# A transformer-mixer prompt kernel: the first chunk's weights and queries, two-matmul dense steps in layer 0, and newly annealed orders of all engines

## The chip, the core and the metric

The kernel runs on one core of a Trainium2 chip. The metric is the device time of one execution in microseconds (us). The engines are TensorE (PE; its weight loads are listed as PEld), VectorE (DVE), ScalarE (ACT), GpSimd (POOL), and SyncE (SP), which issues every DMA of this kernel. Each engine runs its own list of instructions in order and waits on semaphores for the others.

## What is computed

Two equal layers, each with an attention block (A) and a token-mixing MLP (B), on 2048 tokens of width 512, in bf16:

```
def _A_ref(x, wqkv, wo):      # H = 32 heads of 16, window W = 256
    qkv = (x @ wqkv) ...
    scores = einsum("bhqd,bhkd->bhqk", q, k) * Dh ** -0.5
    mask = (i - j >= 0) & (i - j < W)
    p = softmax(where(mask, scores, -1e9))
    return (p @ v) @ wo
def _B_ref(x, w1, b1, w2, b2): # F = 1792
    u = gelu(einsum("bsd,sf->bdf", layernorm(x), w1) + b1)
    return transpose(einsum("bdf,fs->bds", u, w2) + b2)
x = x + _A_ref(layernorm(x)); x = x + _B_ref(layernorm(x))   # twice
```

The MLP mixes tokens: its first matmul sums over all 2048 tokens, its second makes all of them again.

## The kernel before, in words

The tokens are cut into four chunks of 512 (four tiles of 128 each). A chunk is *prepared* (`prepare`, L1052): layer norm statistics on DVE (L686, L688), the inverse root on POOL (L691, L693), normalization on DVE (L697), four PE transposes per tile (L747), whose result DVE or ACT copies out (L731, L733), and then `qkv` (L727): K and Q by `proj` (L756, matmuls at L764, four of 128x512 for each of four blocks o of eight heads), V by `vproj` (L785, 16 small matmuls for each of four sub-blocks, L794). K is written out as `kbd`, two masked copies: in chunk 0 straight by ACT (L773), elsewhere through `stg` and POOL (L780). Q's copy `qT` is a DVE or ACT eviction (L731, L733).

`attention` (L826) takes the four blocks o of a chunk one after the other. For each it makes four (chunk 0) or five *pieces*. A piece is one group of score matmuls (L848, 8 or 12 matmuls in 32-row tiles), two ACT exps of 128x1024 (L860), and masks on DVE (L873, L876). Below, a *step* is one piece, counted from 0; a layer has 76 of them. When a block's pieces are done, a group of 72 or 112 matmuls multiplies the probabilities with V (PV, L894). DVE copies its two banks (`cs`, L938); then follows a normalization by DMA: SP gathers the denominators (L940), copies half the result to other partitions (four DMAs, L944), DVE takes the reciprocal (L947), SP writes it to DRAM (L949) and reads it back spread over partitions (`md`, L952), and POOL multiplies (`oT`, L956). The last block of the last chunk takes a direct path through PE and ACT.

`wo_block` (L962) multiplies the four `oT` of a chunk by `wo` (L966), DVE adds to x, and a twofold layer norm follows. `u_part` (L998) is the MLP's first matmul, one chunk of tokens at a time, added up in SBUF by DVE (L1021, L1024), with GELU on ACT in its last part (L1027); it streams w1 in 256 KB pieces (L981). `y_block` (L1032) is the second matmul (L1035) with w2 (L992). Layer 1's chunks are prepared from `y_block`s of layer 0. The part of the kernel that is neither score nor PV is called *dense*; it fills PE between score groups.

What runs when is fixed while the program is built. `Graph.op` records each operation with its readers, writers and a cost. `schedule` (L350) with `_pick` (L264) is a list scheduler: it places operations on engines by readiness, priority and `RANK`, and inserts warm-up matmuls (L613). Then `reorder` (L420) shifts operations by the offsets in `MOVES` (L35), and `emit` (L429) writes each engine's list with the waits that it needs. A dense group is cut into operations of `STEP` = 4 matmuls (L704, `mm_group` L714, and `u_part`); between two such operations the order may place something else. Each operation signals once, after its last matmul. The last part of `u_part` has steps of one matmul.

SP's list opens with four tiles of x (128 KB each), the 512 KB of V weights, 512 KB of x, K's first 128 KB block, 512 KB of x, Q's first 128 KB block, then the rest.

Of the kernel before, what the change touches and what calls it, by code (L numbers as in the profile page):

```python
# [13 lines left out]
SWITCH = 100.0  # L14
# [6 lines left out]
RANK = (  # L21
    -18, 0, -107, -93, 7, 6, -38, -55, -48, 11, -107, 10, 37, -42, 7, 0, -4, -7, 17, -3, -66, 62, -49, 17, 1, 15,
    -19, 14, -13, 0, 6, 0, -51, 35, 0, 0, 0, 0, 7, -6, 0, 0, 15, 19, -6, -31, 0, -13, -3, 399, 0, 49, -23, 0, -1,
    18, 8, 17, 226, 11, -1, -10, -4, 7, 6, -31, -47, 105, 10, 0, 0, 15, -362, 42, 322, -14, -380, 0, -24, 52, 33,
    -20, -38, -11, 40, 51, -19, 55, -55, 11, 0, 0, 142, -1, 10, -5, 23, 2, 0, 44, 4, 41, 164, 28, -29, 0, 31, 0, 1,
    -46, 60, 13, 0, -18, 0, 15, 8, -122, 460, -486, -53, 10, -5, 0, 7, -20, -3, -14, 0, 12, 0, -12, 1, 0, 0, 0, 0,
    0, -52, 0, 0, 0, 0, 0, 0, 0, 49, -6, -6, -13, -155, -126, 185, -106, -33, -165, 6, -9, 0, -137, -4, 10, 2, 152,
    260, 114, 69, 200, -193, 10, 17, -14, 0, 6, -188, 4, 8, 15, -2, 0, 17, -15, 11, 17, 0, 0, -6, -79, -112, -156,
    0, -15, -114, 238, 115, -376, -10, 2, 0, 17, 0, 4, 6, 12, 0, -28, 0, 0, 117, 31, -17, -17, 0, 0, 473, -6, 86,
    -9, -3, -9, -384, -150, -479, 217, 122, 0, 36, 157, 53, 18, -27, 0, -6, 0, 38, 0, 1, 50, 52, 12, 14, 193, -18,  # L30
    13, 0, -11, 0, 113, 408, -134, 107, -30, -22, -52, 0, 14, 163, 38, 0, 186, -153, -439, 359, -7, 0, -3, 15, -10,
    13, 10, -109, 5, 0, 18, -105, -52, -43, 17, -46, -58, -33, -135, -167, -266, 232, 53, -39, 1, 2, 4, -16, 0, -18,
    -39, 0, 0, 3, 0, -1, 0, 0, 0, 0, 0, 0, 0, 0, 0, 0, 0, 0, 0, 0, 0, 0, 0, 0, 0, 0, 0, 0, 6,
# [3 lines left out]
        3, -1, 2, 5, -2, -4, 0, -2, 1, 3, 1, -1, 1, -6, 0, 0, 0, 0, 1, 1, -2, 0, 1, -1, 0, 0, 0, 0, 2, -1, -1, 1,  # L37
        -1, 0, 1, 1, -2, 2, 0, -2, 0, 0, 0, 2, -1, 1, 3, -3, -1, -1, 0, 0, 0, 0, 0, 0, 0, 0, 0, 0, 0, 0, 0, 0, 0, 0,
        0, 0, 0, 1, -1, 0, 0, 0, 1, -1, 0, 0, 0, 0, 0, 0, 0, 0, 0, 0, 0, 0, 0, 0, 1, -1, 0, 0, 0, 0, 0, 0, 0, 0, 0,
        0, 0, 0, 0, 0, 0, 0, 0, 0, 0, 0, 0, 0, 0, 0, 0, 0, 0, 0, 1, -1, 0, 0, 0, 1, -1, 0, 0, 0, 0, 0, 0, 0, 0, 0,  # L40
        0, 0, 0, 0, 0, 0, 0, 0, 0, 0, 0, 0, 0, 0, 0, 0, 0, 0, 0, 1, -1, 0, 0, 0, 0, 0, 0, 0, 0, 0, 0, 0, 0, 0, 0, 0,
        0, 0, 0, 0, 0, 0, 0, 0, 0, 0, 0, 0, 0, 0, 0, 0, 0, 0, 0, 0, 0, 0, 0, 0, 0, 0, 0, 0, 1, -1, 0, 0, 0, 0, 0, 0,
        0, 0, 0, 0, 0, 0, 0, 0, 0, 0, 0, 0, 0, 0, 0, 0, 0, 0, 0, 0, 0, 0, 0, 0, 0, 0, 0, 0, 0, 0, 0, 0, 0, 0, 1, 1,
        3, 1, -4, -2, 0, 5, 1, 2, 0, -4, 1, -5, 1, 8, 0, 2, 2, 5, -6, -4, 3, -2, 2, -7, -4, 0, 3, 3, 3, -3, 2, -4,
        -4, 0, 0, 0, 21, 21, -1, 2, 2, 2, -6, 1, 3, 3, -8, -8, -8, 4, 4, -2, 7, 2, -4, 1, -5, 3, -6, -14, 1, 1, -16,
        0, 0, 0, 0, 0, 0, 0, 0, 0, 0, 1, -1, 0, 0, 0, 0, 1, -1, 0, 0, 0, 1, 1, -2, 0, 0, 0, 1, 2, -2, -1, 0, 0, 1,
        -1, 0, 0, 0, 0, 0, 0, 1, 1, -2, 0, 0, 0, 0, 0, 0, 0, 0, 0, 0, 0, 0, 0, 0, 0, 0, 0, 0, 0, 0, 0, 0, 1, -1, 0,
        0, 0, 0, 0, 0, 0, 0, 0, 0, 0, 0, 1, -1, 0, 0, 1, -1, 0, 1, -1, 1, -1, 1, -1, 0, 0, 0, 0, 0, 0, 0, 0, 0, 0,
        0, 0, 0, 0, 0, 0, 0, 0, 0, 0, 0, 0, 0, 0, 0, 0, 0, 0, 0, 2, 0, -2, 0, 0, 0, 0, 0, 0, 0, 0, 0, 0, 0, 0, 0, 1,
        -1, 0, 2, 3, -2, -2, -1, 0, 0, 0, 0, 0, 0, 0, 0, 1, -1, 0, 0, 0, 0, 0, 0, 0, 0, 0, 0, 0, 0, 0, 0, 0, 0, 0,  # L50
        0, 0, 0, 0, 0, 0, 0, 0, 0, 0, 1, -1, 0, 0, 0, 0, 0, 0, 0, 0, 0, 0, 0, 0, 0, 0, 0, 0, 0, 0, 0, 0, 0, 0, 1,
        -1, 0, 0, 1, -1, 0, 0, 0, 0, 0, 0, 0, 0, 0, 0, 0, 0, 0, 0, 0, 0, 0, 0, 0, 0, 0, 0, 0, 0, 1, -1, 0, 1, -1, 0,
        0, 0, 0, 0, 0, 0, 0, 0, 0, 0, 0, 0, 0, 0, 0, 0, 0, 0, 0, 0, 0, 0, 0, 0, 0, 0, 0, 0, 0, 0, 0, 3, -1, -1, -1,
        0, 0, 1, 1, 1, -3, 0, 0, 1, -1, 0, 0, 0, 4, 1, 3, 0, 5, 3, -6, -1, -1, -8, 0, 0, 0, 0, 0, 0, 0, 0, 0, 0, 0,
        0, 0, 0, 2, 2, 2, -3, -3, 0, 4, -1, 3, -2, 20, -3, 2, -1, 20, 7, 7, 1, -9, -6, -5, -2, 2, -3, 2, -9, -9, -2,
        14, -8, 1, 7, 7, 2, 2, 15, -9, -9, -9, -7, 3, 3, -2, 3, -3, -8, -13, 4, -3, -2, 4, 1, -4, 2, -1, -6, 2, 2,
        -2, 1, 2, 5, -5, 0, 0, -4, 1, 7, 0, 1, -1, -6, 3, -2, -2, 7, 2, -1, -1, -6, -1, 2, 2, 3, -4, 5, 1, -6, 0, 0,
        -5, 0, 0, 0,
    ),
    (  # L60
        6, -1, 3, 4, 4, 6, 6, 6, 6, 6, 6, 7, 5, 6, 6, 6, 6, -13, 5, 5, 9, -12, -21, 4, 6, 10, -23, 13, 21, -4, 3, 6,
        -6, -23, -6, -1, -4, -6, -2, -1, 4, 0, -3, -1, 4, 12, 0, 0, 11, -6, 6, 12, 0, 2, 4, -2, 4, -12, -8, -8, -6,
        1, 10, 1, 2, 3, -5, -2, 6, 2, 3, -1, 6, 4, -7, 5, -1, -8, 4, 6, -78, -2, 4, 0, -3, 2, 3, 1, 2, -5, 2, 2, -1,
        1, 1, 1, 1, 1, 1, -23, 0, 0, 1, -1, 0, 0, 1, -1, 0, 0, 5, -1, -1, -1, -1, -1, 1, 3, 3, 5, 2, -5, 1, 2, -5,
        1, 1, -9, 1, 1, 2, -3, -1, 2, 2, 2, 3, 1, -4, 2, -7, 1, 1, -3, 2, -1, -1, 1, -1, 1, -1, 0, 1, 1, -2, 1, -1,
        0, 0, 0, 0, 0, 3, -1, 0, -2, 0, 1, 5, 2, 5, -2, -2, 3, -7, -3, -2, 3, 0, -2, 1, -2, 0, 0, 2, 0, -2, 1, -1,
        0, 0, 1, 1, 1, 1, -4, 0, 1, 1, 1, 1, 1, 1, -6, 2, 0, -2, 0, 0, 0, 1, 1, -2, 1, -1, 0, 0, 0, 0, 0, 0, 0, 0,
        0, 0, 0, 1, -1, 1, 1, 2, 2, -1, 1, 2, 0, 2, 2, -1, 4, 1, -13, -2, 3, 0, -3, 2, 2, -1, -4, 0, 1, -1, 4, 0, 4,
        -1, -1, 0, 1, 2, 0, -9, 1, -1, 1, -1, 0, 0, 0, 0, 0, 0, 0, 0, 0, 0, 0, 2, 0, 1, 2, -4, -1, 0, 2, 0, -2, 0,
        0, 0, 0, 0, 0, 0, 1, -1, 2, -1, -1, 0, 0, 3, -1, 0, 1, 2, -4, -1, 2, -1, -1, 0, 3, 3, 0, -2, 1, 1, 1, -7, 0,  # L70
        1, -1, 0, 1, -1, 1, 1, -2, 0, 0, 0, 0, 0, 0, 0, 0, 0, 0, 0, 0, 0, 0, 1, 2, 2, -1, 3, 3, 0, 2, -8, 1, 1, -6,
        0, 0, 0, 0, 3, 0, 0, -3, 2, 0, -2, 1, -1, 0, 0, 0, 0, 0, 0, 1, 1, -2, 3, 0, -2, -1, 0, 1, -1, 0, 1, 1, -2,
        0, 0, 0, 1, -1, 1, 3, 0, 4, -1, 0, -6, 4, -2, 4, -2, -2, 2, -3, 1, 1, 2, 0, 2, 0, 3, -9, 0, -2, 0, 2, 0, 1,
        1, 2, -5, 1, -2, 1, 3, 1, 2, 2, 3, 1, -7, 1, 2, 2, 2, 3, -3, -12, 1, -2, 2, -1, 2, 2, -3, -2, 2, 3, -2, 3,
        3, -2, 2, 3, 1, 3, -9, 0, 1, 3, 1, -1, 3, -12, -1, -1, 0, 0, 0, 0, 0, 0, 0, 1, -1, 1, 2, 0, 2, -4, 1, -2, 1,
        -1, 2, 2, -2, 1, 1, -4, 0, 0, 1, 1, -2, 1, 1, 2, 0, 1, 1, 4, -7, 0, 0, 5, -4, 0, 0, 2, 3, 1, -6, 1, 2, 2, 3,
        -2, 2, -1, 4, 2, -1, 3, 1, 3, 3, 3, 4, -20, -8, 2, -5, 4, 0, 3, 6, 6, -7, 2, 5, 3, 6, 7, 3, 6, 0, 2, 4, -9,
        -14, 4, 2, 0, -15, -20, 2, 0, -2, 0, 1, 1, 2, -3, 1, 2, 0, 1, -5, 0, 1, -1, 1, -1, 8, -1, -1, -1, -1, -1, 0,
        -2, -1, 3, -1, 3, -2, -2, -1, 0, 7, -1, -1, -1, 4, 5, -2, -2, -2, -6, 1, 8, 0, 0, -5, 1, -1, 1, -1, 8, 3,
        -1, -8, 5, -2, 0, -5, -1, -4, 0, 1, 1, 2, 2, 3, 1, 3, -7, -5, -1, 1, 3, 0, -3, -1, 2, -1, 2, 0, 1, -4, 1,  # L80
        -1, 0, 1, 3, -2, 5, -2, -2, 1, -2, 3, 3, 3, -5, 3, -4, 5, 1, 2, -7, -4, -2, 3, 3, -2, 7, -3, 3, 1, 5, 1, -7,
        1, -5, 2, 0, 1, 1, -11, 0, 0, 0, 0, 4, -1, -1, -1, -1, 0, 0, 1, -1, 1, 2, 2, 3, -4, 0, 1, 4, 0, 6, -1, 1, 4,
        -11, 3, -2, -6, -3, 1, 1, 1, -3, 2, -1, 1, -2, 0, 0, 2, 0, -2, 0, 0, 2, 0, -2, 0, 0, 0, 0, 0, 0, 1, -1, 0,
        1, -1, 0,
    ),
    (
        0, 0, 0, 1, -1, 0, 0, 0, 1, -1, 1, -1, 1, -1, 0, 0, 0, 0, 0, 0, 0, 0, 0, 1, 1, -2, 0, 0, 0, 0, 0, 0, 0, 0,
        0, 0, 0, 0, 0, 0, 0, 0, 0, 0, 0, 0, 0, 0, 0, 0, 0, 0, 0, 0, 0, 0, 0, 0, 0, 0, 0, 0, 0, 0, 0, 0, 0, 0, 0, 0,
# [66 lines left out]
class Graph:  # L155
# [956 lines left out]
```

## Time and profile before

| what | value |
|---|---|
| median of 5 runs | 479.53 us (479.18 to 480.55) |
| profiled execution | 479.49 us, span of its instructions 477.8 us |
| first score matmul, first exp | 15.61 us, 16.70 us |
| exps of layer 0 | 152, from 16.70 to 172.5 us |
| L860, all exps | 304, 283.9 us busy |
| L1012 and L1035, the MLP's matmuls | 448 each, 106.9 and 103.7 us busy |
| ACT waits for scores, 240 to 400 us | 20.5 us in 36 waits |

A row of instructions gives engine, line, output and inputs, shape and count; times are from the span's start. "Idle before" is what the engine stood still ahead of them, with the instruction that ended the wait. A busy time of overlapping matmuls is a union, and a single matmul's duration (380 ns for 128x512) is longer than the distance to the next one, so that sums over streams of matmuls have to use distances from start to start. The chain of waits is the chain of work that ended last, followed back from the end.

### The profile page before, as it was taken

The page shows a single profiled execution, that of the slowest core. Times are in us where ns is not written, and L with a number is a line of the kernel's source. Part 1 is how long each engine was busy: PE and PEld are TensorE (multiplying, and loading weights), DVE is VectorE, ACT ScalarE, POOL GpSimd, SP SyncE. Part 2 cuts the span into 40 slices and gives each one's busy share as a digit, 9 for nine tenths or more (in the row PEclk, how much of TensorE's full clock was granted, in tenths as well). Part 3 has the DMA queues.
Part 4 walks back from the last instruction along what each step waited for, and adds up shares of the span by engine and source line. Part 5 has one row for each costly group of instructions (what it writes and reads, how often), then busy time and mean ns, then how long its engine had stood idle before and what let it go on. Part 6 is the DMA issues. An engine that isn't in the chain of part 4 may idle for free.

```text
span 477.8 us, 15704 instructions
## 1 busy us (share of the span) xinstructions
PE 435.8 (91%) x6830; PEld 207.4 (43%) x6830; DVE 368.0 (77%) x746; ACT 326.9 (68%) x372; POOL 127.2 (27%) x197
## 2 busy tenths in 40 slices
PE   7889867879989799999989899999998999999997
PEld 4355433443333444455344354444543444444443
DVE  6998989789988978763786788989977786952222
ACT  1899998898999960636998798788897882061000
POOL 3222452363521213020012513352473131200000
PEclk9999999999999999999999999999999999999999
DMA  8513232222252443231044224241224445524654
GB/s 245 153 38 93 70 96 53 80 85 59 66 155 83 139 104 110 67 104 51 23 135 116 63 74 121 73 131 32 81 70 135 124 132 142 144 77 138 178 169 133
DMA packets 83993, 49.47 MB, mean 104 GB/s; under 512 B 14676, under 2 KB 78164, under 8 KB 83924
## 3 DMA queue, kind: packets, MB, share of 16 engines
q1 hardware_dynamic: 83924, 48.46, 35.9%
q8 instruction: 54, 0.88, 0.8%
q14 instruction: 15, 0.12, 0.1%
HBM read 41.43 MB, written 2.59 MB: 92 GB/s over the span
## 4 chain that ended last, share of the span: by engine, by line
PE 59%; ACT 21%; DVE 9%; issue 3%; DMA 3%; SPq 2%; POOL 2%; POOLq 0%
ACT pt L860 20%; PE PS L1035 17%; PE PS L1012 15%; PE PS L894 6%; PE PS L764 5%; PE PS L848 5%; PE PS L966 4%; PE PS L794 4%; DVE pt L876 3%; DMA w1b<-in_B_w_dram 2%; DVE cs L938 1%; PE PS L613 1%; ACT kbd L773 1%; SPq L992 1%; SPq L944 1%
## 5 line engine op out<-in xcount | busy, mean ns | idle before, releaser
L860 ACT ACTIVATE pt<-PS 128x1024 bf16<-128x1024 f32 (+1 forms) x304 | 283.9, 1026 | 33.4 <-PE PS L848 31.1
L1012 PE MATMUL PS<-xh_sb,w1b 128*128 128x512 bf16 x448 | 106.9, 380 | 3.7 <-DMA w1b<-in_B_w_dram 0.9
L1035 PE MATMUL PS<-ub,w2b 128*128 128x512 bf16 x448 | 103.7, 380 | 0.0
L848 PE MATMUL PS<-qT,kbd 32*128 32x64 bf16 (+4 forms) x1632 | 60.5, 243 | 21.0 <-ACT pt L860 10.0
L1012 PEld LDWEIGHTS PS<-xh_sb,w1b 128*128 128x128 bf16 x448 | 39.9, 98 | 56.3 <-issue 5.3
L764 PE MATMUL PS<-xhT,wqkv 128*128 128x512 bf16 x256 | 62.4, 381 | 1.4 <-DVE vt L731 0.9
L956 POOL TENSOR_TENSOR oT<-cs,md 128x512 bf16<-128x512 f32 x30 | 38.4, 1279 | 94.4 <-DMA cs<-cs 52.1
L1035 PEld LDWEIGHTS PS<-ub,w2b 128*128 128x128 bf16 x448 | 41.2, 98 | 50.2 <-issue 4.0
L1024 DVE TENSOR_TENSOR ub<-PS,ub 128x512 f32<-128x512 f32 x70 | 46.0, 684 | 17.6 <-PE PS L1012 17.2
L876 DVE TENSOR_TENSOR pt<-pt,ldm 128x1024 bf16<-128x1024 bf16 (+1 forms) x80 | 56.8, 723 | 2.4 <-ACT pt L860 2.2
L848 PEld LDWEIGHTS PS<-qT,kbd 32*128 32x128 bf16 x1632 | 23.3, 92 | 76.8 <-ACT pt L860 43.1
L780 POOL TENSOR_SCALAR kbd<-stg,par 128x512 bf16<-128x512 bf16 x48 | 38.9, 820 | 64.3 <-DVE stg L731 49.5
L938 DVE COPY cs<-PS 128x512 f32<-128x512 f32 x60 | 39.1, 684 | 17.2 <-PE PS L894 15.7
L1040 DVE SCALAR_TENSOR_TENSOR x_sb<-PS,bcol,x_sb 128x512 bf16<-128x512 f32 x32 | 23.3, 745 | 35.6 <-PE PS L1035 35.5
L1027 ACT ACTIVATE ub<-ub,bcol 128x512 bf16<-128x512 f32 x28 | 18.5, 713 | 45.7 <-DVE ub L1024 45.7
L894 PE MATMUL PS<-pt,vt 64*18 64x64 bf16 (+4 forms) x3040 | 39.8, 242 | 6.5 <-ACT pt L860 2.7
L873 DVE TENSOR_TENSOR pt<-pt,ldm 128x512 bf16<-128x512 bf16 (+1 forms) x104 | 40.9, 416 | 3.9 <-ACT pt L860 3.7
L686 DVE BATCH_NORM_STATS2 stats<-x_sb 128x6 f32<-128x512 bf16 x64 | 43.1, 682 | 0.6 <-DMA x_sb<-in_A_x_dram 0.2
L691 POOL TENSOR_SCALAR rstd<-agg 128x2 f32<-128x2 f32 (+1 forms) x40 | 9.4, 235 | 121.3 <-DVE agg L688 120.2
L894 PEld LDWEIGHTS PS<-pt,vt 64*18 64x18 bf16 x3040 | 31.0, 84 | 16.9 <-ACT pt L860 6.3
L764 PEld LDWEIGHTS PS<-xhT,wqkv 128*128 128x128 bf16 x256 | 21.9, 98 | 30.3 <-issue 3.9
L794 PE MATMUL PS<-wqkv,xhT 128*64 128x256 bf16 x512 | 33.6, 275 | 1.5 <-issue 0.5
(54 smaller groups left out, 327.3 us busy)
## 6 DMA issues: line engine op xcount, KB each, us to landing
w2b<-in_B_w_dram SPq DMA_DIRECT2D x112, 128.0 KB, 2.3
w1b<-in_B_w_dram SPq DMA_DIRECT2D x56, 256.0 KB, 3.5
md<-rscr SPq DMA_DIRECT2D x30, 256.0 KB
cs<-cs SPq DMA_DIRECT2D x120, 32.0 KB, 2.8
out_dram<-x_sb SPq DMA_DIRECT2D x16, 128.0 KB, 1.8
x_sb<-in_A_x_dram SPq DMA_DIRECT2D x3, 512.0 KB
wqkv<-in_A_wqkv_dram SPq DMA_DIRECT2D x2, 384.0 KB, 5.3
x_sb<-in_A_x_dram SPq DMA_DIRECT2D x4, 128.0 KB
```

Of the source, the lines that this page charges most:

```text
L686: op("vector", lambda e, t=t: e.bn_stats(stats[:, t, :], x_sb[:, t, :]), reads=[f"x{t}"], writes=[f"st{t}"], cost=dve_cost(512))
L764: mm_group(ft, 4, lambda e, c: e.matmul(PS[:, ft.slot, :], lhsT=wqkv[:, c, which * 512 + o * P:which * 512 + (o + 1) * P], rhs=xhT[:, tx.s ...
L794: last = e.matmul(PS[64 * hf:64 * hf + 64, ft.slot, sc * 256:(sc + 1) * 256], lhsT=xhT[:, tx.slot, c, tok:tok + 64], rhs=wqkv[:, c, 1024:1 ...
L848: last = e.matmul(PS[:, bank(r), c0 * 64:(c0 + nb) * 64], lhsT=kbd[32 * r:32 * r + 32, tkk.slot, jj, :, :].rearrange("p h n -> p (h n)"), ...
L860: return e.activation(pt[:, tp.slot, 2 * u:2 * u + 2, 0:n], PS[:, b0:b0 + 2, 0:n], ACTF.Exp, scale=SMSCALE)
L873: return e.tensor_tensor(v, v, msk.unsqueeze(1).to_broadcast([P, 4, w]), op=ALU.mult)
L876: return e.tensor_tensor(v, v, msk.unsqueeze(1).unsqueeze(1).to_broadcast([P, 4, k, w]), op=ALU.mult)
L894: last = e.matmul(PS[32 * r:32 * r + 18, tO[h].slot, q0 * 64:(q0 + nb) * 64], lhsT=vt[64 * h:64 * h + 64, tvv.slot, jj, 4 * o + r, :], rhs ...
L938: op("vector", lambda e, tO=tO[h], tc=tc, h=h: e.tensor_copy(cs[:, tc.slot, h], PS[:, tO.slot, :]), reads=[tO[h]], writes=[(tc, h)], cost= ...
L1012: out_ = e.matmul(PS[:, tu.slot, :], lhsT=w1b[:, tw.slot, s, tt * P:(tt + 1) * P], rhs=xh_sb[:, 4 * m + s, :], start=(n == 0 and s == 0), ...
L1024: op("vector", lambda e, tu=tu, ft=ft: e.tensor_tensor(uacc(ft), PS[:, tu.slot, :], uacc(ft), op=ALU.add), reads=[tu] + uk(ft), writes=uk( ...
L1035: mm_group(ft, NFT, lambda e, fc: e.matmul(PS[:, ft.slot, :], lhsT=w2b[:, tws[fc // W2F].slot, fc % W2F, k * P:(k + 1) * P], rhs=uT(fc), s ...
```

## The change

The list scheduler is gone: `_pick`, `RANK`, the class limits of PSUM and the automatic warm-up insertion are removed. In its place `follow(ORDER)` takes five written lists of operation numbers, one for each engine, and only works out which buffers each operation gets and so what it must wait for. `MOVES` is kept with new numbers. The cut of dense groups becomes two matmuls in layer 0 and stays four in layer 1. `load_x` and `load_w` are declared in another order. A K copy of chunk 0 may be made by ACT or DVE (the new lists leave all of them on ACT). Chunk 0's layer norm takes tiles in pairs.

```diff
-RANK = (
...
+ORDER = (
...
 MOVES = (
...
-    def schedule(self):
+    def follow(self, orders):
...
+                o = lists[e][ptr[e]]
+                if o.ndeps:
+                    continue
+                t = free[e] + (SWITCH if e == "tensor" and o.mode != mode else 0.0)
+                t = max(ready[o.idx], t)
...
-        load_x(0, 1)
-        load_x(1, 2)
+        for t in range(4):
+            load_x(t, t + 1)
         load_w(4, 5)
-        load_x(2, 3)
-        load_x(3, 4)
         load_w(0, 1)
...
-        STEP = 4
+        STEP = (2, 4)
...
-            for k0 in range(0, n, STEP):
-                k1 = min(n, k0 + STEP)
+            st = STEP[g.layer]
+            for k0 in range(0, n, st):
+                k1 = min(n, k0 + st)
...
-            cls, st = ("big", 1) if last else ("small", STEP)
+            cls, st = ("big", 1) if last else ("small", STEP[g.layer])
...
-                    if m == 0:
-                        ln_block([t], False)
-                    elif t % 2:
+                    if t % 2:
                         ln_block([t - 1, t], False)
...
-        g.schedule()
+        g.follow(ORDER)
         g.reorder(MOVES)
```

In the resulting instruction lists PE, DMA and exp counts are the same as before. POOL has eight instructions fewer (the inverse roots of chunk 0 in pairs), and one Q eviction is on DVE in place of ACT. PE begins with the same 13 warm-up matmuls; then 16 V matmuls, eight transposes, 16 V, K0 and Q0, 16 V and the first scores, where before there were 24 V, eight transposes, 40 V, K0, Q0 and K1 ahead of them. SP's list opens with four tiles of x, the V weights, 512 KB of x, K's first block, one w2 piece of 128 KB and Q's first block. Later in layer 0 the macro order of pieces, PV, output projection and MLP is the same, with other portions of dense work between scores; in layer 1 nearly all fillers are as before.

## Prediction

> **What bounds the kernel now.** I read the page first, then the busy time of each engine by stage, then what ScalarE (ACT) waits for, and last the order of TensorE (PE) instruction by instruction.
>
> ```profile
> span 477.8 us, 15704 instructions
> PE 435.8 (91%) x6830; PEld 207.4 (43%) x6830; DVE 368.0 (77%) x746; ACT 326.9 (68%) x372; POOL 127.2 (27%) x197
> PE 59%; ACT 21%; DVE 9%; issue 3%; DMA 3%; SPq 2%; POOL 2%; POOLq 0%
> ```
>
> PE is busy for 91% of the span, but that is an average over stages. The four stages (layer 0's attention, layer 0's token MLP, layer 1's attention, last MLP) differ:
>
> ```profile
> 16.00:172.00 156.00, 131.72 (x2863) 63.60 (x2860) 141.19 (x290) 145.15 (x163) 55.37 (x76) 1.00 0.31 85
> 172.00:236.00 64.00, 63.76 (x564) 30.27 (x562) 42.67 (x85) 31.59 (x43) 7.29 (x17) 1.00 0.28 77
> 236.00:398.00 162.00, 151.24 (x2948) 72.20 (x2946) 135.57 (x277) 135.42 (x147) 55.67 (x74) 1.00 0.36 101
> 398.00:478.00 80.00, 75.67 (x350) 33.87 (x348) 36.35 (x61) 10.11 (x15) 4.29 (x9) 1.00 0.47 138
> ```
>
> The columns are length, then busy PE, weight load, VectorE (DVE), ACT, GpSimd (POOL), clock, DMA share, GB/s. In layer 0's attention ACT is the fullest: 145.15 of 156, so 10.85 us idle, with DVE 14.8 and PE 24.3 idle. In the two MLP stages and in layer 1 PE is the fullest (idle 0.24, 10.8 and 4.3). The clock is full throughout. What ACT waits for in layer 0's attention:
>
> ```profile
> ACT pt L860 <- PE PS L848: 9.7, 13, 1.8
> ACT pt L860 <- PE PS L894: 0.6, 1, 0.6
> ```
>
> Nearly all of its idle time ends with a score matmul of PE: PE is not short of time there, it is late, because it is in order and stands in other work when ACT needs scores. So the sum that matters is what PE does between one group of scores and the next, against the time of the two exps per group. The timeline prices the pieces:
>
> ```profile
> 36.88 1.90 PE L764 MATMUL PS<-xhT,wqkv 128*128 128x512 bf16 x8
> 38.71 0.40 PE L848 MATMUL PS<-qT,kbd 32*128 32x320 bf16 x8
> 39.04 1.90 PE L764 MATMUL PS<-xhT,wqkv 128*128 128x512 bf16 x8
> 40.88 0.34 PE L848 MATMUL PS<-qT,kbd 32*128 32x320 bf16 x8
> 41.15 1.04 PE L764 MATMUL PS<-xhT,wqkv 128*128 128x512 bf16 x4
> 42.14 0.40 PE L848 MATMUL PS<-qT,kbd 32*128 32x320 bf16 x8
> ```
>
> From start to start: scores 0.33, eight dense matmuls 1.84, four about 0.97. Dense streams elsewhere run at 0.216 each, so 8 x 0.216 = 1.73 and a change from dense to row tiles costs 0.107. By the same differences, 16 V matmuls are 0.99 and a probabilities-times-V group (PV) is 0.95 in chunk 0 and about 1.3 after. Exps follow each other every 0.904 us when scores are there, so a step has 1.81 us of cover. A step's sum that is under this lets ACT catch up; one that is over makes ACT idle once its half step of buffered scores is used.
>
> **The change part by part.** Both orders have the same PE instructions (6,832), DMAs (411) and exps (304). Removed: eight small POOL instructions (layer norm of chunk 0 in pairs: per pair 0.26+0.78 for 2x(0.20+0.56)), off the path. Moved: one Q eviction from ACT (0.59) to DVE (0.69). Everything else is order, and the size of layer 0's dense steps.
>
> *Two-matmul steps.* They let a step hold six matmuls in place of eight and four. Laying both orders side by side and summing each of the steps 2 to 75 of layer 0 by the prices above (fillers that differ, samples):
>
> ```
> steps   before                 sum         after           sum
> 11,12   qk8 | qk4              2.17 1.30   qk6 | qk6       1.73 1.73
> 20      PV tr8 v16             2.72        PV tr8 v8       2.26
> 46      u8                     2.17        u6              1.73
> 53      u4 PV                  2.49        PV              1.52
> 58      u4 PV u4               3.46        u2 PV           2.06
> 28,34   wo4 PV wo4 | PV u8     3.46 3.36   wo8 PV | same   3.36 3.36
> ```
>
> Steps over 2.1 us fall from 25 to 15, and the excess over 1.81, summed over all steps, from 15.2 to 9.8. The measured idle time of ACT is 10.85 for an excess of 15.2, a ratio of 0.71; with it the new order leaves 7.0, a gain of 3.9. From the other side, ACT's idle times one by one: 0.6 at step 20, 0.96 at 46, 0.51 at 53, 1.02 at 58 and two small ones (0.35) stand at steps that got lighter, 3.4 together; the 1.80 and 1.62 at steps 28 and 34 stay. Of these 3.4 some 2.5 should go, since the lightened steps still exceed 1.81 at 20 and 58. I take 3.2, with 1.0 and 4.5 as ends.
>
> What the finer steps cost: the order of PE has 163 changes of tile mode in layer 0 for 155, and 179 for 176 in layer 1. Weighted by kind that is 0.7 us of PE time in all, most of it where PE has 24 us to spare. [...] The chain of waits has both granularities side by side:
>
> ```profile
> 409.61 12.09 PE PS L1012 x56
> 433.78 40.59 PE PS L1035 x188
> ```
>
> L1012 signals here after every single matmul, L1035 after every fourth; both take 0.216 each. The row decides: no cost per signal.
>
> *The head.* 16 of the 64 V matmuls, K1 and Q0's ACT eviction move behind the first scores, and Q0's weights pass the 512 KB load of x.
>
> ```profile
> 12.74 2.76 PE L764 MATMUL PS<-xhT,wqkv 128*128 128x512 bf16 x12
> 13.81 1.27 ACT L773 ACTIVATE kbd<-PS,par 128x512 bf16<-128x512 f32 x2 [0.38 <-PE PS L764]
> 14.97 0.59 ACT L733 CAST qT<-PS 128x512 bf16<-128x512 f32 x1
> 15.61 0.40 PE L848 MATMUL PS<-qT,kbd 32*128 32x320 bf16 x8
> 16.70 1.94 ACT L860 ACTIVATE pt<-PS 128x1024 bf16<-128x1024 f32 x2
> ```
>
> K0 can start after 32 V matmuls, near 11.4. The K weights keep their place in SP's queue. Q's are issued near 4.7 as before with 384 KB less ahead; at 5.9 to landing they are there by 10.6, before Q0 at 12.3. K0's two ACT writes then run 12.5 to 13.7; Q0's copy on DVE waits for four layer-norm statistics (4 x 0.69, from about 11.1) until 13.8 and ends at 14.5. Scores start near 14.5 for 15.61, exps near 15 for 16.70. But ACT then still owes K1 (1.27), done before the first exp today. Net 0.5 to 1.0; I take 0.7. If the weights came 1 us late this part would be nothing.
>
> *SP's queue.* Two 256 KB loads of w1 now stand between the first group's denominator gather and its copies (2 x 0.5 us), the 512 KB of wo moves behind the fourth gather; these only delay the normalization of chunk 0, which a rival prices.
>
> *Layer 1 and the MLPs.* Dense steps stay at four there. Layer 1's excess falls from 29.2 to 28.1, but PE bounds it and PE's work is the same. The last MLP has the same sum (76.1). I take 0.2 for all of it, ends -1.0 (loss) and 2.0.
>
> **The sum.** 3.2 + 0.7 + 0.2 = 4.1 us off the profiled span of 477.8 gives 473.7. That execution took 479.49 (1.7 around the span), the median of the runs is 479.53, so the same 4.1 gives 475.4.
>
> **The rivals.** *DVE takes over.* DVE has 14.8 us idle in layer 0's attention, in stretches much less (12 us windows with 11.5 busy at 108 and 120), and nothing is taken from it; masks and evictions then come late, and PV and scores wait for them. For it: PE's waits on DVE there (2.6 us for qT before scores, 1.0 for stg). Against: the gaps to be closed are at PE's long steps. Half of the 3.9 and 0.7 more for late evictions are lost: 475.4 + 2.0 + 0.7 = 478.1.
>
> *Slower: the normalization stalls PE at the output projection of chunk 0.*
>
> ```profile
> 70.52 1.30 POOL L956 TENSOR_TENSOR oT<-cs,md 128x512 bf16<-128x512 f32 x1 [2.42 <-DMA cs<-cs]
> 71.92 1.02 PE L966 MATMUL PS<-wo_sb,oT 128*128 128x512 bf16 x4 [1.10 <-ACT pt L860]
> ```
>
> The last oT of chunk 0 ends at 71.82 and wo starts 0.1 later: no slack today. The new order puts all eight matmuls ahead of PV at step 28; while they wait, PV, the next scores and so ACT stand. Ten SP issues (about 0.6 each, wo_sb 0.9) lie between the last gather and its broadcast, for seven now, but none after it for two now, so I expect equality to 1 us. If each of chunks 0 to 2 comes late by 1.8 us, 5.4 is lost, and with 4.1 gained the time is 480.8. It decides from about 4 us of lateness in all.
>
> *Layer 1 gains too.* PE waits there for masks and fetches some 10.8 us; if 4 of them go as well: 471.4.
>
> **How the numbers follow.** The forecast (473.5 to 477.5) has 0.60, DVE 0.20, slower 0.10, layer 1 too 0.10. A measurement of this kernel tells about 0.2% (1 us) from no change. DVE's case straddles that bound at 478.6: half of it is faster, half the same. Faster 0.60+0.10+0.10 = 0.80, same 0.10, slower 0.10. The range 471.0 to 479.5 leaves out the slower case and a little below.
>
> **What would show it.** ACT's wait for L848 in layer 0's attention falls from 9.7 to 6 or 7; the first exp starts near 15; wo's first start follows the last oT of chunk 0 without a new wait over 1 us; layer 1 from first to last exp stays within 1 us; the last MLP likewise. It is wrong if ACT's idle time stays near 10.8 with DVE as releaser, or if PE's waits on oT or on w1 grow.

## The result, and the profile after

The new kernel takes 476.9 us (median of 44 runs, 474.1 to 483.1), the kernel before 478.6 in the same rounds (79 runs): a ratio of 0.9963, 95% interval 0.9948 to 0.9977. That is 1.7 us faster where 4.1 was forecast: sign and engine were right, the size is less than half. That 476.9 lies in the likeliest range (473.5 to 477.5) is in part luck: the forecast was laid from a median of 479.53 over five runs, and the same kernel has 478.61 here; from 479.53, a gain of 1.7 would give 477.8. The profiled execution took 476.42 us with a span of 474.7, 3.1 under that of before; a second profile of the same kernel has 475.8. So one pair of traces shows more than the medians do, and a stage has to be compared over several.

The page after, the same three lines as before:

```profile
span 474.7 us, 15701 instructions
PE 435.5 (92%) x6830; PEld 206.5 (43%) x6830; DVE 370.3 (78%) x747; ACT 326.2 (69%) x371; POOL 126.6 (27%) x189
PE 62%; ACT 17%; DVE 14%; DMA 2%; issue 2%; POOL 2%; SPq 0%; POOLq 0%
```

The busy sums are the same. On the chain of the end, ACT lost 4 points and DVE won 5. The stages (columns as in the prediction) and what ACT waits for in layer 0's attention:

```profile
15.00:169.00 154.00, 133.85 (x2880) 64.09 (x2878) 139.59 (x292) 144.12 (x162) 55.95 (x77) 1.00 0.31 86
169.00:233.00 64.00, 63.28 (x568) 30.21 (x567) 43.86 (x86) 31.30 (x43) 7.44 (x14) 1.00 0.29 83
233.00:395.00 162.00, 149.94 (x2936) 71.98 (x2934) 138.51 (x275) 135.57 (x147) 55.25 (x74) 1.00 0.36 96
...
ACT pt L937 <- PE PS L925: 8.3, 12, 2.7
ACT pt L937 <- PE PS L971: 0.7, 1, 0.7
```

ACT is still the fullest engine there, but its wait for scores fell from 9.7 to 8.3, not to 6 or 7, and the longest is now 2.7 (1.8 before). In the head, the first scores and the first exp come at 12.79 and 13.38 for 15.61 and 16.70, ahead of the forecast:

```profile
9.96 1.90 PE L836 MATMUL PS<-xhT,wqkv 128*128 128x512 bf16 x8
11.04 1.41 ACT L848 ACTIVATE kbd<-PS,par 128x512 bf16<-128x512 f32 x2 [1.38 <-PE PS L836]
12.01 0.67 DVE L803 CAST qT<-PS 128x512 bf16<-128x512 f32 x1
12.79 0.40 PE L925 MATMUL PS<-qT,kbd 32*128 32x320 bf16 x8
13.38 1.03 ACT L937 ACTIVATE pt<-PS 128x1024 bf16<-128x1024 f32 x1
```

The same marks in every trace of this study, in us. The length of step k is the time from the first score matmul of step k-1 to that of step k. The head is counted from PE's first transpose to the scores of step 10, since that transpose comes at 6.3 to 7.4 without any change of order (the warm-up matmuls ahead of it come 0.43 us apart at first, for 0.216 in later streams, and the records of the granted clock begin, at full speed, at 5.2 to 8.2 us). "ACT idle" is what ACT stands still ahead of exps between layer 0's first and last; "half" is a stretch of 3.4 us at a granted clock of 0.5 within the stage.

| kernel | head | steps 10 to 75 | ACT idle | steps 76 to 151 | step 151 to end |
|---|---|---|---|---|---|
| before | 31.3 | 131.2 | 10.6 | 169.3 | 86.8 |
| before, 90 signals | 31.9 | 132.4 (half) | 11.8 | 169.0 | 88.0 |
| before, edges shifted | 31.9 (half) | 130.2 | 9.8 | 166.6 | 87.1 |
| new | 30.6 | 128.8 | 9.2 | 168.5 | 88.4 |
| new, again | 30.7 | 129.5 | 9.8 | 168.5 (half) | 88.4 |
| POOL edges | 30.8 | 130.7 | 11.2 | 167.9 | 86.9 |
| step 65 swapped | 30.8 | 130.9 | 11.4 | 167.2 | 88.5 |
| steps put back | 31.2 | 132.2 | 12.4 | 169.3 (half) | 88.4 |
| K2 in the head | 32.3 | 131.6 (half) | 12.4 | 167.2 (half) | 88.4 |
| end edge, cs first | 30.9 | 128.8 | 9.4 | 166.0 | 86.9 |
| the same, again | 30.6 | 128.9 | 9.4 | 167.4 | 86.9 |
| and SP order | 30.6 | 128.9 | 9.5 | 166.6 | 86.9 |
| end edge, cs first, shift 104 | 30.8 | 126.5 | 7.1 | 168.4 (half) | 86.9 |
| end edge, cs first, shift 16 | 30.6 | 131.6 (half) | 12.0 | 170.3 (half) | 86.9 |

The new order gains 0.4 to 1.3 in the head (0.9 in the mean) and 0.3 to 2.4 in layer 0 (traces with this order, or with one small edit of it, are up to 2.1 us apart). It loses 1.5 at the end against the first trace of before, wherever the end is left as it was; the old order's own traces have 86.8 to 88.0 there, the longest with a wait of 1.9 us for a load of w1 (0.7 in the first).

### The profile page after: what moved, and what is told of

It reads as the page before. It is cut to its first block, busy times and chain, and to the rows that moved or that the text cites. A ratio compares the mean times of both kernels' runs of the same rounds, so it can differ in the third digit from the quotient of the medians.

```text
span 474.7 us, 15701 instructions
## 1 busy us (share of the span) xinstructions
PE 435.5 (92%) x6830; PEld 206.5 (43%) x6830; DVE 370.3 (78%) x747; ACT 326.2 (69%) x371; POOL 126.6 (27%) x189
## 4 chain that ended last, share of the span: by engine, by line
PE 62%; ACT 17%; DVE 14%; DMA 2%; issue 2%; POOL 2%; SPq 0%; POOLq 0%
PE PS L1112 18%; PE PS L1089 17%; ACT pt L937 16%; PE PS L836 6%; PE PS L971 6%; PE PS L925 5%; PE PS L871 4%; PE PS L1043 4%; DVE cs L1015 2%; DVE xh_sb L768 2%; DVE pt L950 2%; DVE pt L953 2%; DMA w1b<-in_B_w_dram 1%; DVE stats L757 1%; DVE x_sb L1117 1%
## 5 line engine op out<-in xcount | busy, mean ns | idle before, releaser
L937 ACT ACTIVATE pt<-PS 128x1024 bf16<-128x1024 f32 (+1 forms) x304 | 283.5, 1039 | 30.9 <-PE PS L925 28.4
L836 PE MATMUL PS<-xhT,wqkv 128*128 128x512 bf16 x256 | 63.6, 381 | 0.0
L953 DVE TENSOR_TENSOR pt<-pt,ldm 128x1024 bf16<-128x1024 bf16 (+1 forms) x80 | 58.1, 736 | 2.3 <-ACT pt L937 1.7
L1033 POOL TENSOR_TENSOR oT<-cs,md 128x512 bf16<-128x512 f32 x30 | 40.3, 1347 | 69.7 <-DMA cs<-cs 51.6
L857 POOL TENSOR_SCALAR kbd<-stg,par 128x512 bf16<-128x512 bf16 x48 | 40.1, 845 | 69.8 <-DVE stg L803 69.6
L950 DVE TENSOR_TENSOR pt<-pt,ldm 128x512 bf16<-128x512 bf16 (+1 forms) x104 | 39.7, 403 | 5.0 <-ACT pt L937 4.9
L871 PE MATMUL PS<-wqkv,xhT 128*64 128x256 bf16 x512 | 34.8, 276 | 1.2 <-DVE x_sb L1117 0.4
L1043 PE MATMUL PS<-wo_sb,oT 128*128 128x512 bf16 x128 | 32.7, 381 | 1.7 <-POOL oT L1033 1.4
```

Source lines behind the costliest of these rows:

```text
L836: mm_group(ft, 4, lambda e, c: e.matmul(PS[:, ft.slot, :], lhsT=wqkv[:, c, which * 512 + o * P:which * 512 + (o + 1) * P], rhs=xhT[:, tx.s ...
L871: last = e.matmul(PS[64 * hf:64 * hf + 64, ft.slot, sc * 256:(sc + 1) * 256], lhsT=xhT[:, tx.slot, c, tok:tok + 64], rhs=wqkv[:, c, 1024:1 ...
L937: return e.activation(pt[:, tp.slot, 2 * u:2 * u + 2, 0:n], PS[:, b0:b0 + 2, 0:n], ACTF.Exp, scale=SMSCALE)
L950: return e.tensor_tensor(v, v, msk.unsqueeze(1).to_broadcast([P, 4, w]), op=ALU.mult)
L953: return e.tensor_tensor(v, v, msk.unsqueeze(1).unsqueeze(1).to_broadcast([P, 4, k, w]), op=ALU.mult)
L1043: mm_group(ft, 4, lambda e, o, i=i, ft=ft: e.matmul(PS[:, ft.slot, :], lhsT=oT[:, tos[o][0].slot, i * P:(i + 1) * P], rhs=wo_sb[:, o, :], ...
```

## The experiments

Each kernel is set against runs of the kernel before on the same chip; all ratios are to it. `move(engine, operations, place)` puts operations ahead of another in an engine's list, `edge(a, b)` makes b wait for a.

### The new kernel again

> The changed kernel once more, unaltered, to see what of the stage times repeats. Theory (the gain is in the orders): score step 0 to step 75 of layer 0 within 0.3 us of the 152.9 of the first profile, step 76 to 151 within 0.5 of 168.5, and the first score matmul at 12.8, or up to 1 us later [...]. Rival (much of the difference is the luck of one execution): stage times that differ by more than 1 us from the first profile.

477.24 us for 479.81, ratio 0.9956 (0.9937 to 0.9975): the gain repeats. Of the stage times neither side came true as put: steps 0 to 75 are 153.5 for 152.9, between the 0.3 and the 1 us that were named, and steps 76 to 151 are 168.5 again. Single steps differ by more: step 34 took 4.46 us (5.73 in the first), step 65 3.39 (2.77).

### Does a signal cost PE time? (before, 90 signals)

```diff
-                        last = mk(e, k)
+                        last = mk(e, k)
+                        if lay == 0 and k == k0 + 1:
+                            last.then_inc(extra, 1)
```

and the same after the second matmul of each MLP operation of layer 0: 90 increments of a semaphore on which nobody waits.

> The kernel before, with one more semaphore increment after the second matmul of each of layer 0's 90 dense groups of four; nobody waits for it. By the row (streams of single-matmul steps run at 0.216 us per matmul as those of four do): no change, within 0.3 us by stage. [...]

480.49 us for 479.81, ratio 1.0005 (0.9986 to 1.0024). The interval ends 1.2 us (0.0024 of 479.81) above no change, 13 ns for each of the 90. So no cost of the signals of two-matmul steps shows in these streams of 128x512 matmuls. Their further changes of tile mode (0.7 us by the prediction) were not tried alone.

### DVE and POOL at two places (POOL edges)

```diff
+        edge(516, 444)
+        edge(2081, 2188)
```

At step 34 one POOL product (`oT`) waits for a mask, at the end one waits for the last normalization of DVE (`xh_sb`).

> The changed kernel with two more waits on GpSimd: the oT multiplication at 82.7 us waits for the mask that DVE does at the same time, and the pair of oT multiplications at 384 us waits for the three normalizations of xh on DVE. Theory ([...] a 0.69 us mask took 1.75 and two 0.40 us normalizations took 1.36 each): the mask takes 0.69 again, step 34 falls from 5.73 to about 4.7, PE's wait of 1.45 us on a DVE copy after step 151 goes; 2.0 to 2.5 us less in all against the changed kernel. Rival (the wait moves on, to the slots of PSUM or to w1): DVE is faster but step 34 and the end of layer 1 keep their lengths within 0.3 us.

476.19 us, ratio 0.9926 (0.9897 to 0.9955), 1.0 us under the repeat of the new kernel in the same rounds, where 2.0 to 2.5 were expected. The end is shown. Kernel before:

```profile
391.77 0.81 DVE L697 TENSOR_SCALAR xh_sb<-x_sb,agg,rstd 128x512 bf16<-128x512 bf16 x2
...
390.83 1.27 POOL L956 TENSOR_TENSOR oT<-cs,md 128x512 bf16<-128x512 f32 x1
...
391.32 3.63 PE L1012 MATMUL PS<-xh_sb,w1b 128*128 128x512 bf16 x16
```

New kernel:

```profile
384.54 2.96 DVE L768 TENSOR_SCALAR xh_sb<-x_sb,agg,rstd 128x512 bf16<-128x512 bf16 x3
...
384.26 2.76 POOL L1033 TENSOR_TENSOR oT<-cs,md 128x512 bf16<-128x512 f32 x2 [0.84 <-DMA cs<-cs]
...
388.15 3.63 PE L1089 MATMUL PS<-xh_sb,w1b 128*128 128x512 bf16 x16 [1.45 <-DVE ub L1098]
```

and with the edge:

```profile
387.16 1.05 DVE L768 TENSOR_SCALAR xh_sb<-x_sb,agg,rstd 128x512 bf16<-128x512 bf16 x3
...
388.29 2.50 POOL L1033 TENSOR_TENSOR oT<-cs,md 128x512 bf16<-128x512 f32 x2 [2.23 <-DVE xh_sb L768]
...
389.23 2.98 PE L1089 MATMUL PS<-xh_sb,w1b 128*128 128x512 bf16 x13
```

In the kernel before, POOL's one product is nearly over when the normalizations start. In the new one two of the three lie beside POOL's two products: the three take 2.96 us (1.36, 1.35 and 0.40), and 1.05 without the products; the copies `ub` behind them come late, and PE waits 1.45 us for the PSUM that they free. With the edge the wait is gone and the end is 86.9 for 88.4, as in the five later traces with this edge. At step 34 the mask took 0.68 us for 1.75, as expected, and yet the step took 5.71 as before. Whatever holds PE there is not the mask.

### The early output projection (step 65 swapped)

```diff
+        move("tensor", [737, 738], 880)
```

The new order has `wo` at step 65, where before had MLP matmuls and `wo` one step later. New kernel, then with the MLP matmuls in front again:

```profile
PE PS L1043 <- POOL oT L1033: 1.4, 1, 1.4
```

```profile
PE PS L1089 <- DMA w1b<-in_B_w_dram: 1.3, 1, 1.3
```

> The changed kernel with one pair of operations exchanged in PE's order: at steps 65 and 66 of layer 0 the four MLP matmuls go ahead of the four output projections, as in the kernel before. Theory (the output projection was pulled in front of its oT): PE's wait of 1.40 us on oT at 145 us goes and score step 75 is reached 0.9 to 1.4 us earlier. Rival (the slack is lost elsewhere): step 65 is shorter, but a later step gives it back, and step 75 moves by less than 0.4 us.

478.73 us, ratio 0.9985 (0.9962 to 1.0009): a miss. The wait for `oT` became one for a load of w1, which stands on SP's queue behind the next gather. Step 65 took 3.54 us.

### The steps put back

The dense work of steps 45 to 52 and 57 to 70 goes back to the steps in which it was before; the lists, cut:

```diff
+        arrange("tensor", 194, [791, 649, 650, 677, 678, 807, ...
+            948, 952, 702, 705, 859, 703, 706, 956, 712, 713, 960, ...
+        arrange("vector", 263, [835, 860, 861, 704, 707, 951, ...
```

> The new kernel, with the dense work of layer 0's steps 45 to 52 and 57 to 70 put back step by step as it was before (step 46 has eight MLP matmuls again, 57 none, 58 eight around PV, wo stands at step 66 and not at 65), in two-matmul operations as they are; 27 operations of PE and some 20 of DVE move by one step. First theory (the prediction's: lighter steps were worth 3.2 us, 2.0 of it at steps 46 and 58): some 2 us slower than the new kernel, ACT idle between layer 0's first and last exp 2 us more than the 9.2 and 9.8 of the two traces of the new order. Second theory (what 46 and 58 gain is given back at 48, 56, 57, 59 and 65, which took that work): within 0.7 us, steps 45 to 70 as long in sum as in the new kernel (49.2 us in its trace). Rival to both (the early wo is the worst of it): faster by 1 us.

480.13 us, ratio 1.0037 (1.0018 to 1.0057), 0.7 to 0.8% over the new kernel. Steps 10 to 75 are 2.7 to 3.4 us longer than in the two traces of the new kernel, and ACT idles 2.6 to 3.2 more. By the number that is the first theory's side, but the trace does not bear it out. Step 58 took 5.24 us where it took 4.08 in the kernel before:

```profile
131.87 1.36 PE L971 MATMUL PS<-pt,vt 64*18 64x128 bf16 x112
133.17 1.04 PE L1089 MATMUL PS<-xh_sb,w1b 128*128 128x512 bf16 x4
135.81 0.37 PE L925 MATMUL PS<-qT,kbd 32*128 32x128 bf16 x8 [1.61 <-DVE ub L1101]
```

The scores wait for DVE's additions of the MLP, which I had put behind the copies of PV. ACT idles 3.00 us there (1.02 in the kernel before), and not at all at step 46, though that step has its eight MLP matmuls back. Nor is this the old order again: steps 45 to 70 take 56.1 us, but 53.1 to 53.7 in the three traces of the old order and 52.1 to 54.6 in the seven with the new one. So this run shows that its own mixture is slow; what the lighter steps are worth it does not show. The second theory, that the neighbours give back what 46 and 58 gain, fits the sums for steps 45 to 70, which are equal in the mean (53.3 old, 53.2 new).

### Part of the head undone (K2 in the head)

```diff
+        move("tensor", [103, 104], 185)
+        move("scalar", [105, 106], 187)
```

> The new kernel with part of its head undone: K2's eight matmuls (1.73 us) go ahead of the first scores and its two ACT writes (1.27 us) ahead of the first exps. If the first exp's time is what counts: first exp 1.3 to 1.8 us later and the whole 1.5 us slower. If ACT's sum of work counts (what it does before the first exp it does not owe afterwards): first exp as late, but by the tenth step no more than 0.5 us are left of it, and the time is within 0.5 us.

478.69 us, ratio 1.0002 (0.9975 to 1.0028). The edit moved four matmuls, not the eight of the expectation (two operations of two), 0.97 us with a wait of 0.30 for their weights ahead. Counted from the first transpose, the first exp is 1.9 to 2.5 us later than in the traces of the new order, and the head to step 10 is 32.3 for 30.6 to 31.2. So most of the delay stays: the first exp's time counts, nearer to the first theory, though some of it is given back. The ratio is 0.4% over the new kernel's, but the intervals touch, and this trace has two half-speed stretches. It shows what can follow a stall in PE's clock (PE busy in the second column, clock third from the end):

```profile
83.70:87.11 3.41, 1.42 (x113) 1.13 (x111) 3.41 (x6) 2.61 (x3) 3.41 (x4) 1.00 0.02 5
87.11:90.52 3.41, 3.41 (x16) 1.04 (x18) 1.83 (x4) 0.00 (x0) 1.15 (x2) 0.50 0.13 33
```

After 3.41 us with PE busy for 1.42 come 3.41 us at half speed. The eight MLP matmuls of step 34 fall into them:

```profile
86.96 3.49 PE L1089 MATMUL PS<-xh_sb,w1b 128*128 128x512 bf16 x8 [1.99 <-ACT pt L937]
```

They took 3.49 us for 1.89 in the new kernel's trace, after a stall of 1.99, and step 34 was 7.6 us long.

### What holds PE at step 34 (end edge, cs first; and SP order)

```diff
+        edge(2081, 2188)
+        move("vector", [499, 498], 516)
```

and in a second kernel also

```diff
+        move("vector", [867], 718)
+        move("sync", [868], 729)
```

> The new kernel with two edits: at the end the second oT product on POOL waits for the normalization on DVE that it slowed before (alone worth 1.5 us in the traces so far), and at step 34 DVE copies the two banks of PV ahead of the mask that stood before them. If step 34's wait (1.5 to 1.7 us of PE for cs) is DVE's order: step 34 falls from 5.7 or 4.5 to about 4 and the time is 1 us under that of the end edit alone, some 2.5 under the new kernel. If it is the late mask's PV that counts (it comes at step 38), the gain comes back as a longer step 38 and only the end's 1.5 stays.

> As the kernel before it in this list, and at steps 58 to 61 the reciprocal of the third block of chunk 2 goes one MLP addition earlier on DVE, and its write to DRAM goes ahead of a w1 load and of one copy on SP. If the DMA chain of the normalization sets step 65 (wo waited 1.4 and 2.0 us for oT), the write leaves 0.9 us earlier, md and oT likewise, and step 65 falls from 2.8 to 3.5 us to about 1.9 to 2.5. If a landing that other loads slow sets it (the w1 load behind came 1.3 us late when it stood in front), step 65 stays at 2.8 or more.

474.76 us, ratio 0.9922 (0.9893 to 0.9951), and 474.07, 0.9908 (0.9876 to 0.9940). Both lie under the new kernel's 0.9963. The end edge gave its 1.5 again (86.9), but step 34 still took 5.6 to 5.7 us, and step 65 was short (1.85 and 1.74) with and without the change on SP; in a repeat of the first kernel, below, it took 2.50. So cs is not what PE waits for at 34, and for SP's order nothing is shown. In the kernel before, the same eight matmuls waited less:

```profile
86.06 1.90 PE L1012 MATMUL PS<-xh_sb,w1b 128*128 128x512 bf16 x8 [0.55 <-DVE xh_sb L697]
```

The first trace and the second of the unchanged new kernel decide what does not hold PE there:

```profile
81.17 1.36 PE L971 MATMUL PS<-pt,vt 64*18 64x128 bf16 x112 [0.42 <-ACT pt L937]
84.26 1.89 PE L1089 MATMUL PS<-xh_sb,w1b 128*128 128x512 bf16 x8 [1.73 <-ACT pt L937]
...
78.20 5.67 ACT L937 ACTIVATE pt<-PS 128x1024 bf16<-128x1024 f32 x6
```

```profile
81.44 1.36 PE L971 MATMUL PS<-pt,vt 64*18 64x128 bf16 x112 [0.42 <-ACT pt L937]
83.24 1.90 PE L1089 MATMUL PS<-xh_sb,w1b 128*128 128x512 bf16 x8 [0.44 <-ACT pt L937]
...
78.47 5.67 ACT L937 ACTIVATE pt<-PS 128x1024 bf16<-128x1024 f32 x6
```

The profile names ACT. But in the second trace the MLP matmul starts at 83.24, while ACT's last exp ends at 84.14: it needs no more than the one before it, which in the first trace had ended at 82.95, 1.3 us before 84.26. DVE's last normalization had ended at 82.91, 1.35 us before, and no load landed within 3.3 us; DVE's mask was still running in both when PE started. Other stalls lie inside one group of matmuls, where nothing is waited for, as at step 62 with the POOL edges:

```profile
140.35 0.92 PE L971 MATMUL PS<-pt,vt 64*18 64x128 bf16 x78
142.24 0.61 PE L971 MATMUL PS<-pt,vt 64*18 64x64 bf16 x34 [0.97 <-issue]
```

What the stalled places have in common is their number. Counting PE's instructions (weight loads, matmuls, waits of its sequencer) from the start, the stalls of the new order at steps 34, 59, 62, 69, 119 and 132 (each trace has some of them) end at instructions 2754, 4800, 5057, 5568, 10177 and 11200: each some 192 to 194 over a multiple of 256. The first trace has 54 instruction packets of 16 KB, PE's instructions in it are 13,818, which makes one packet for every 256, and these stalls end 2.2 to 2.9 us after the start of such a packet. A PV group is 224 instructions in 1.36 us, so after one the next block is soon needed.

### Shifting the block edges (end edge, shift 104; shift 16)

```diff
+        parts = [8, 8, 8, 8, 4, 4, 4, 4, 4, 4, 4, 4]
...
+            k = parts.pop(0) if parts else 1
+            w = 512 // k
+            for j in range(k):
...
+                last = e.matmul(PS[:, t.slot, j * w:(j + 1) * w], lhsT=zero[:], rhs=rhs, start=True, stop=True)
```

Warm-up matmuls are cut into narrower ones: the same columns, 104 PE instructions more. With `parts = [2] * 8` there are 16 more.

> The kernel with the two edits (end edge, cs ahead of the mask) unaltered, as the base for the two that follow. In four traces PE stood 1.6 to 2.0 us at step 34 with everything that it needs done, and what started again was the same instruction each time, number 193 of a row of 256 of PE's own. First theory (PE's instructions arrive in blocks of 256, some 3.3 to 4.6 us after the block before is entered, and a PV group runs through nearly one block in 1.4 us): step 34 is near 4.5 or near 5.6, nothing between. The time is again 0.991 to 0.994 of before.

> The same with the first twelve warm-up matmuls cut into four or eight narrower ones: 52 matmuls, 104 PE instructions more, the same columns, so no time of its own (0.2 us at most). All later edges of PE's blocks come 104 instructions earlier. Blocks theory: no stall at step 34 (5.6 to about 4.0) and none at 59, 62, 69; new ones, 0.4 to 1.6 us each by the distances in the trace, at steps 29 and 39 and one in layer 1; summed over all block edges the intervals that are shorter than 4.5 us lack 5.3 us for 10: 1 to 2 us faster than the base. If step 34 waits for something else (cs, exps, a load): step 34 stays at 5.6 and the time within 0.3 us.

> The same with eight warm-up matmuls cut in two: 16 PE instructions more, no time of their own. Blocks theory: the edges come to lie at the end of PV groups; the intervals shorter than 4.5 us lack 14.5 us for 10, those shorter than 3.4 us 4.6 for 2: 2 to 4 us slower than the base, with stalls at steps 34 (PV's last matmuls), 57 to 59 (1.2 to 2.3), 68 (1.4 to 2.5), 134 and 141. If PE's blocks do not matter: within 0.3 us.

Base 474.77 us, ratio 0.9938 (0.9915 to 0.9961); shift 104 473.96, 0.9906 (0.9879 to 0.9932); shift 16 476.44, 0.9947 (0.9925 to 0.9970). The whole times move the way that the blocks say, but by less than the least that I expected (0.8 us for 1 to 2, and 1.7 for 2 to 4), and each interval overlaps the base's. The traces say more. With the shift of 104 step 34 is 4.47 us (5.95 in the base):

```profile
82.57 1.36 PE L978 MATMUL PS<-pt,vt 64*18 64x128 bf16 x112 [0.42 <-ACT pt L944]
84.61 1.67 PE L1096 MATMUL PS<-xh_sb,w1b 128*128 128x512 bf16 x7 [0.67 <-DVE xh_sb L775]
...
ACT pt L944 <- PE PS L932: 6.0, 12, 1.4
ACT pt L944 <- PE PS L978: 0.8, 1, 0.8
```

Steps 10 to 75 take 126.5 us, 2.4 under the base, and ACT idles 7.1. Of the new stalls that were forecast, those at 29 and 39 are there with 0.3 us each, and the one in layer 1 is 1.39 us at step 124, where an edge now follows a PV group (4.23 for 2.84). With the shift of 16 an edge falls behind PV and scores of step 58, and PE stands still longer than anywhere in the other traces:

```profile
129.15 1.36 PE L978 MATMUL PS<-pt,vt 64*18 64x128 bf16 x112
130.45 0.40 PE L932 MATMUL PS<-qT,kbd 32*128 32x128 bf16 x12
133.60 1.67 PE L1096 MATMUL PS<-xh_sb,w1b 128*128 128x512 bf16 x7 [2.75 <-DVE pt L960]
```

Of the other places where I expected stalls with this shift, step 141 has 0.5 us, and steps 34 (4.46), 68 and 134 have none; step 131, which I had not named, has 1.8. The forecast of single places is thus half right. What it lacks is when a block comes: the stalls of the unshifted traces end 3.5 to 7.9 us after the instruction 256 places ahead had started, and not 3.3 or 4.5.

### Is the gain only where the edges fall? (before, edges shifted)

The kernel before with the same 104 instructions.

> The kernel before, unaltered but for its first twelve warm-up matmuls cut into four or eight narrower ones: 104 PE instructions more, so that the edges of PE's blocks of 256 come as much earlier. By the distances in its trace the intervals between edges lack 5.6 us for 9.9 at 4.5 us a block, and 1.7 for 1.7 at 3.4. First theory (the two orders differ by their steps, the edges take from each in its own places): 0 to 1.5 us faster than before, some 476.5 to 478.5, and still 2 us or more over the new order with the same shift. Rival (most of what the new order gains is where its edges fall): 2.5 us faster or more, level with the new kernel.

476.88 us for 478.93, ratio 0.9966 (0.9944 to 0.9987): as much as the whole change brought. The 2.05 us lie between the two theories, over the 1.5 of the first and under the 2.5 of the rival. Its steps 98, 111, 119 and 141, three of which had stalls of 0.4 to 1.0 us ended 2.4 to 2.5 us after an instruction packet, are 2.9 us shorter together. The longest, at step 141, stood as this line in the waits of the kernel before, in the middle of a group of scores, and is gone:

```profile
PE PS L848 <- issue: 1.0, 1, 1.0
```

The rival falls for layer 0, by one trace of each: at this shift the new order takes 126.5 us for steps 10 to 75 and the old 130.2. For the whole time it does not fall so far: the new kernel without a shift (0.9963) is level with the old one with it.

## Why the prediction was right and where it was not

*Two-matmul steps, 3.2 us.* The mechanism held in part. Three of the named steps ran shorter, as their sums said (46 from 3.19 to 1.92, though other traces of the old order have 2.35 and 2.98; 53 from 2.75 to 1.83; 58 from 4.08 to 2.17). Step 20 did not (3.52 to 3.58), though it lost eight V matmuls. The size failed: steps 10 to 75 gained 0.3 to 2.4 us over the seven traces with this order or a small edit of it (1.7 in the mean). ACT's idle time ahead of exps, by step, shows where:

| step | 20 | 28 | 34 | 43 | 46 | 47 | 53 | 58 | 59 | 62, 63 | 65 |
|---|---|---|---|---|---|---|---|---|---|---|---|
| before | 0.6 | 1.8 | 1.6 | 0.7 | 1.0 | 0.8 | 0.5 | 1.0 | 0 | 0.8 | 0 |
| new | 0.5 | 0.9 | 2.7 | 0 | 0 | 0.5 | 0 | 0.2 | 0.8 | 1.3 | 0.6 |
| end edge, cs first, shift 104 | 0.5 | 1.0 | 1.4 | 0 | 0 | 0.5 | 0 | 0.2 | 0.2 | 1.1 | 0 |

At the four places that were named (20, 46, 53, 58) the new kernel wins 2.4 us, close to the 2.5 of the prediction. It loses 3.0 at 34, 59, 62, 63 and 65, and wins 0.9 at 28, 0.7 at 43 and 0.3 at 47, for which nothing was forecast. The term that failed is the conversion of sums into ACT's idle time: it allowed for the cover of a step and for nothing that PE waits for outside a sum. Step 34 gives back 0.9 us (4.80 to 5.73; 1.73 us of waiting for instructions, 0.55 before), step 65 0.9 by its wait for `oT`; the work that steps 46 and 58 gave away makes others longer, so that steps 56 to 61 take 12.4 us for 11.9. The same omission also hid a gain. Steps 42 and 43 have the same work on PE in both orders and took 4.93 us before and 3.66 after; two waits are gone that stood there before:

```profile
PE PS L894 <- DVE stg L731: 1.0, 1, 1.0
PE PS L764 <- DVE vt L731: 0.9, 1, 0.9
```

With the edges shifted ACT idles 7.1 us, where the prediction had worked out 7.0, and 9.8 in the old order with the same shift. That the totals agree is partly luck: the places do not, since 20 stayed and 28, which was to stay, fell. What the experiments show is that the new order's layer 0 is 3.7 us shorter than the old one's at this shift; that the lighter steps bring all of this is not shown. I had read stalls on fetches in layer 1 (0.4, 0.5 and 1.0 us in the trace of before, each ended some 2.5 us after an instruction packet's start) but put no price on any in layer 0.

*No cost per signal.* Right as far as it was measured: 90 signals, ratio 1.0005, and the interval ends at 1.0024 (1.2 us).

*The head, 0.7.* Right in size: 31.3 to 31.9 us to step 10 became 30.6 to 30.9. First scores at 12.79, not 14.5, are 1.0 of an earlier first transpose in that execution (6.36 for 7.37), and Q0 and K0 came sooner than I had summed; the first ten steps, with K1's two ACT writes in them, gave 1.0 back.

*Layer 1 and the MLPs, 0.2.* Layer 1 gained 0.8 in both traces of the new kernel, within the range. It was not "the same" all the same: at step 134 PE waits longer for DVE's copy `stg`, which is late behind a mask that took 1.50 us beside an `oT` product. The step takes 2.0 to 2.1 us in ten of the eleven traces of the new order (1.25 in the first) and 0.9 in the old. In the second trace:

```profile
346.43 0.40 PE L925 MATMUL PS<-qT,kbd 32*128 32x128 bf16 x12 [1.66 <-DVE stg L803]
```

The end failed: "the last MLP has the same sum" is true of PE's matmuls, and the end still lost 1.5 us in each trace without the edge, because two POOL products now fall on DVE's normalizations. One edge gives it back. The prediction compared the PE lists of this stage, and not what else had moved on DVE and POOL.

*The rivals.* DVE does not take over as the engine of ACT's waits; it costs at the end and at step 134. The normalization does not stall `wo` of chunk 0 (0.28 us, for ACT), which was the place named, but that mechanism came at step 65, chunk 2, with 0.2 to 2.0 us in eight of the nine traces that have `wo` there. What makes `oT` so late in some executions was not found.

*The sum.* Of the 4.1 forecast, the head brought 0.9, layer 0 1.7 and layer 1 0.8; the end took 1.5 and the stretch between the layers 0.4. That leaves 1.5, for 1.7 by the medians. A further part may be PE's clock: in 52 runs of the new kernel there were 0.8 half-speed stretches a run by their mean clock, in 129 runs of before 0.4. At 1.7 us a stretch (half of 3.4, an estimate) this would be 0.7 us; as a cause it is argued from the clocks, not shown by a run. Five of the seven stretches in traces of the new order follow the wait at step 134. Where no stretch was met (a mean clock of 0.999 or more) the new kernel's repeat has 476.7 (4 runs) and the kernel before in the same rounds 479.3 (24 runs), 2.6 us apart; but such runs may also be those with the shorter stalls.

The best versions are the new kernel with the end edge, cs first, and either the SP order or the shift of 104: 0.9908 and 0.9906, which these runs do not tell apart.

## What to carry to other kernels

Where two orders differ by a few microseconds, count PE's instructions as well as its time: where the edge of a block of 256 fell in or behind a PV group (224 instructions in 1.36 us), it cost 0.3 to 2.75 us here in the places that stalled, and a change anywhere ahead moves every later edge. Try the same order with a shift of the edges before crediting the order. When a new order leaves PE's work in a stage unchanged, compare what now runs side by side on DVE and POOL in it. One trace of each is not enough for a stage that varies by 2 us.

## What the runs showed of the hardware

*PE's blocks.* 54 packets of 16 KB for 13,818 instructions of PE, one for every 256; the stalls at an edge in or behind a PV group took 0.3 to 2.75 us. The same edge cost 1.73 and 0.44 us in two executions of one kernel: the packet started 2.4 or 0.9 us after the instruction 256 places ahead of the stalled one, and PE went on 2.4 or 2.7 us later. Why it starts when it does, the traces do not show.

*DVE beside POOL.* A bf16 mask of 128x1024 takes 0.69 us, and 1.75 beside an `oT` product; a normalization 0.40, and 1.36. Some 30 DVE operations were stretched by over 0.1 us in the new kernel's trace, 15 in that of before, all of them beside a POOL operation. With the POOL edges, where POOL's products wait, the mask at step 34 took 0.68 again and the three normalizations of the end 1.05 together, for 2.96. Why DVE is slower beside POOL, the traces do not show.

*The clock.* All nine half-speed stretches in these traces (granted clock 0.50 for 3.4 us) follow 3.41 us in which PE was busy for 1.2 to 1.62: 1.54 with 90 signals, 1.60 in the new kernel's second trace, 1.59 with the steps put back, 1.42 and 1.58 with K2 in the head. PE stood still in them for up to 2.0 at a time (1.99 ahead of the stretch from 87.11). Three stretches as idle, counted in steps of 3.41 us from where the records of the clock begin, were not followed by half speed (in the new kernel's first trace the one from 80.5 us, with 1.62), so the busy time alone does not tell in these numbers.
